# Ten one-row token tiles, a regrouped last weight and earlier row sums in an attention plus soft-MoE kernel

## The chip, the cores and the metric

The kernel runs on one core of one Trainium2 chip. The core has five engines that run side by side: TensorE (PE, with its weight loads shown apart as PEld), VectorE (DVE), ScalarE (ACT), GpSimd (POOL) and SyncE (SP), and sixteen DMA engines that carry what SP and POOL issue. The metric is the device time of one execution in microseconds (us). Four runs of the kernel before gave 177.15 to 180.34 us, median 179.23 us.

## What is computed

The reference, cut to what matters:

```python
# attention, q, k, v: (8, 8, 576, 64): scores masked to a window of 32 (heads 0-3)
# or to every 4th of 128 positions (heads 4-7), softmax, times v
x = attn_out.transpose(0, 2, 1, 3).reshape(4608, 512)
# soft mixture of experts: phi (512, 32), w1 (8, 512, 1024), w2 (8, 1024, 512)
logits = x @ phi                                # 4608 tokens x 32 slots
d = softmax(logits, axis=0); slot_input = d.T @ x           # 32 x 512
for e in range(8):                               # four slots per expert
    h = maximum(slot_input[e] @ w1[e], 0); slot_out[e] = h @ w2[e]
c = softmax(logits, axis=1)
return (c @ slot_out)                            # 4608 x 512, float32
```

The output is 4608 x 512 float32, 9.44 MB. Both softmaxes use the same exponentials: the kernel keeps exp(logits) transposed, slots by tokens (`expT`). The sum over tokens scales `slot_out` when it is evicted to `so_sb`; the sum over slots, one number per token (the row sum), becomes its reciprocal `rtok` and scales each output row.

## The kernel before

The program is a list of operations (`op(...)`), each with an engine, the buffers that it reads and writes, an estimated cost and a key. A planner (`Prog.schedule`) places them one by one: on each engine it takes, among the operations that could start within 0.1 us of the earliest, the one with the lowest key. SP and POOL keep the order in which the operations were written down. The order found so is emitted as a fixed instruction stream per engine with semaphore waits. While PE would wait within planned time 118 to 141, the planner puts in filler matmuls (line 1014) whose result nobody reads.

Eight attention units (`load_unit`, `st_T`, `st_S`, `st_V`, `st_P`, `st_X`, `st_L`) take the first 130 us or so. POOL issues their loads, and between and behind them the loads of `w1` and `w2` (`wload`, line 473), which turn float32 into bfloat16 on the way. All of these go through one software queue, in order. The second weight `w2` comes in pieces named in `W2`: (expert pair, first and last row of 16, first and last column). `p0`, `p1`, `p2` are whole pairs; the last pair is cut into `p3a` (4 rows, all 512 columns, loaded early, ahead of `p0`), `p3b` and `p3c` (the other 12 rows, columns 0 to 255) and `p3d` and `p3e` (those rows, columns 256 to 511). The last four are the last loads of the kernel.

Behind the attention PE folds the slot inputs (line 827, out of `psA_sb`), multiplies by `w1` (line 846), transposes the hidden layer (line 866) and multiplies by `w2` piece by piece as it lands (line 894), into two accumulators of 256 columns, one for each half of the output's columns. Between the `w2` pieces stand two other things: the 36 row-sum matmuls (`rsum`, line 921), one per 128 tokens, placed behind `p1` (`after=[mid]`), and seven matmuls (`keep`, line 910, `WARM = 7`) behind `p2` whose result nobody reads. When the first half's accumulator is complete, DVE scales it into `so_sb` (line 935).

The output is made in token tiles. A tile of n rows per partition has 128 n tokens, partition p holding n tokens in a row. `TILES` is (1, 2, 3, 5, 4, 8, 13). The first four tiles (`NSPLIT = 4`) are made in two halves of 256 columns: first all four with the left half, then all four with the right half; the last three take 512 columns at once. For each row PE multiplies `expT` by `so_sb` (line 972); DVE (line 991, or line 983 for two rows at once) or ACT (line 989) scales by `rtok` and evicts into a staging buffer that was a weight's home, and when all rows of a tile are there SP issues its store (line 1005). So there are 11 stores: 8 halves, whose pieces in DRAM are 256 columns long (1 KB), and three wide ones, whose pieces are a partition's whole share (8, 16 and 26 KB). SP waits at the end for all of them (line 1036).

Of the kernel before, what the change touches and what calls it, by code (L numbers as in the profile page):

```python
# [7 lines left out]
AluOp = mybir.AluOpType  # L8
# [44 lines left out]
class Op:  # L53
    n = 0
# [75 lines left out]
class Prog:  # L130
# [7 lines left out]
    def op(self, e, fn, r=(), w=(), a=(), alloc=(), cost=0.5, key=0.0, mode="f",  # L138
           sem=None, nbytes=0, nd=0, nq=1, ni=2, after=()):
        o = Op(e, fn, cost, key, mode)  # L140
        deps = list(after)
        for b in r:
            deps += b.ready
        for b in w:
            b.fresh()
            deps += b.prev
        for b in a:
            deps += b.prev
        seen = set()
        for d in deps:  # L150
            if d.id not in seen:
                seen.add(d.id)
                o.deps.append(d)
        for b in r:
            b.reads.append(o)
        for b in list(w) + list(a):
            b.ready.append(o)
        o.wr = [b for b in list(w) + list(a) if b.pool is not None]
        for b in list(r) + list(w) + list(a):
            if b.pool is not None and b not in o.touch:  # L160
                b.left += 1
                o.touch.append(b)
        o.alloc = list(alloc)
        o.sems = sem
        o.ni = ni + 2
        o.dma = nbytes / 435e3 + 0.011 * nd / 16 + 0.022 * nq
        self.ops.append(o)
        return o
# [149 lines left out]
def bass_dilated_sliding_attn__then__soft_moe_slots_kernel(  # L318
# [12 lines left out]
    op = P.op  # L331

    def sb(name, shape, dt=BF16):
        return A(nc.sbuf_tensor(name, shape, dt))

    WARM = 7
    TURNS = ((32, 0, 4), (32, 1, 4), (32, 2, 4), (16, 3, 8), (15, None, 0), (6, 39, 8), (2, None, 0),
             (2, 87, 8), (6, None, 0), (4, 103, 8), (2, 7, 8), (2, None, 0), (2, 23, 8))
    W2 = {"p3a": (3, 0, 4, 0, 512), "p0": (0, 0, 16, 0, 512), "p1": (1, 0, 16, 0, 512),
          "p2": (2, 0, 16, 0, 512), "p3b": (3, 4, 14, 0, 256), "p3c": (3, 14, 16, 0, 256),  # L340
          "p3d": (3, 4, 14, 256, 512), "p3e": (3, 14, 16, 256, 512)}
    NPT, NVN, NXB, NXT, NET = 6, 5, 5, 4, 2
    WD = sb("WD", [128, 7, 4096])
    stg = sb("stg", [128, 3, 9216])
# [40 lines left out]
    def tile(pool, size=1):  # L385
        t = Buf(pool)
        t.size = size
        return t
# [51 lines left out]
    def home(ap, al, name):  # L440
        b = Buf()
        b.al = al
        HOME[name] = (ap, b)
        b_home.append((ap, b))
# [31 lines left out]
    for e in range(7):  # L476
        home(WD[:, e, :], [], f"w1{e}")
    home(stg[:, 2, 0:4096], [b_stg[2]], "w17")
    home(stg[:, 2, 4096:6144], [b_stg[2]], "p3a")
    home(stg[:, 2, 6144:8704], [b_stg[2]], "p3b")  # L480
    home(stg[:, 0, :], [b_stg[0]], "p0")
    home(stg[:, 1, 0:8192], [b_stg[1]], "p1")
    TTf = TT[:].rearrange("p a x -> p (a x)")
# [357 lines left out]
    for hh in range(2):  # L841
        def pe(t, hh=hh):
            for c in range(4):
                for hi in range(2):
                    for j in range(4):
                        i_ = t.matmul(pair(hp)[32 * j:32 * j + 32, hh, :], siT[:, 512 * hi + 128 * c + 32 * j:
                                                       512 * hi + 128 * c + 32 * j + 32],
                                      w1v[2 * j + hi][:, c, 512 * hh:512 * hh + 512],
                                      start=(c == 0 and hi == 0), stop=(c == 3 and hi == 1))
            return i_  # L850
# [9 lines left out]
    for p_ in range(2):  # L860
# [11 lines left out]
        def ev(en, p_=p_, ht=ht):  # L872
            d_ = hT[:, 8 * p_:8 * p_ + 8, :].rearrange("p c (j i) -> p c j i", j=4)[:, :, :, 0:8]
            s_ = bank(ht)[:, 0:256].rearrange("p (c j i) -> p c j i", c=8, j=4)
            return en.activation(d_, s_, ACTF.Copy) if p_ == 0 else en.tensor_copy(d_, s_)
        op("act" if p_ == 0 else "dve", ev, r=[ht], w=[b_hT[p_]], cost=0.35, key=K1)

    TILES = []
    NSPLIT = 4
    POOLS = False  # L880
    for n in (1, 2, 3, 5, 4, 8, 13):
        TILES.append((128 * sum(x[1] for x in TILES), n))
    tok = [[expT[:, t0 + j:t0 + j + n * 127 + 1:n] for j in range(n)] for t0, n in TILES]
    rcol = [sum(n for _, n in TILES[:i]) for i in range(len(TILES))]
# [30 lines left out]
               ni=2 * WARM, key=K1 + 3.9, after=[last_])  # L915
    rs = tile(psum, 1)

    def rsum(t):
        for o, (_, n) in enumerate(TILES):
            for j in range(n):  # L920
                i_ = t.matmul(bank(rs)[:, rcol[o] + j:rcol[o] + j + 1], tok[o][j], rowm[:],
                              start=True, stop=True)
        return i_
    op("pe", rsum, r=b_expT + [b_rowm], w=[rs], alloc=[rs], cost=2.0, key=K1 + 3, ni=72,
       after=[mid])
    op("dve", lambda vv: vv.reciprocal(rtok[:], bank(rs)[:, 0:N_TOK // 128]), r=[rs], w=[b_rtok],
       cost=0.2, key=K1 + 1)

# [10 lines left out]
    for o_ in P.ops[-2:]:  # L939
# [3 lines left out]
    WDf = WD[:].rearrange("p e x -> p (e x)").bitcast(F32)  # L943
    w17f, p0f, p1f = [HOME[x][0].bitcast(F32) for x in ("w17", "p0", "p1")]
    wdh = [f"w1{e}" for e in range(7)]
    STAGE = [(w17f[:, 0:512], ["w17"]), (w17f[:, 512:1536], ["w17"]), (p0f[:, 0:1536], ["p0"]),
             (p0f[:, 1536:4096], ["p0"]), (p1f[:, 0:2048], ["p1"]), (WDf[:, 6656:10752], wdh),
             (WDf[:, 0:6656], wdh)]
    nev = 0
    for o, h_ in [(o, h_) for h_ in range(2) for o in range(NSPLIT)] + [(o, None) for o in range(NSPLIT, 7)]:  # L950
        t0, n = TILES[o]
        ost = STAGE[o][0].rearrange("p (j f) -> p j f", j=n)
        sl = slice(0, 512) if h_ is None else slice(256 * h_, 256 * h_ + 256)
        ob = Buf()
        for x in STAGE[o][1]:
            ob.prev = ob.prev + HOME[x][1].ready + HOME[x][1].reads
        k1 = K1 + 30 + o + 10 * (2 if h_ is None else h_)
        w = sl.stop - sl.start
        for j0 in range(0, n, 2):
            po = tile(psum, w // 256)  # L960
            kk = k1 + 0.1 * j0
            b_po = [Buf(), Buf()]

            def slot(j, po=po, w=w):
                if w == 512:
                    return pair(po)[:, j, :]
                return bank(po)[:, w * j:w * j + w]
            m = min(2, n - j0)
            for js in [range(m)] if w == 256 else [(j,) for j in range(m)]:
                def pe(t, o=o, slot=slot, j0=j0, js=js, sl=sl):  # L970
                    for j in js:
                        i_ = t.matmul(slot(j), tok[o][j0 + j], so_sb[:, sl], start=True, stop=True,  # L972
                                      skip_group_check=True)
                    return i_
                j = js[0]
                p0 = op("pe", pe, r=(b_so if h_ is None else b_so[h_:h_ + 1]) + b_expT, a=[po],
                        w=[b_po[j]], alloc=[po] if j == 0 else [], after=[p0] if j else [],
                        cost=0.22 if h_ is None else 0.15 * m, key=kk + 0.01 * j, ni=2 * len(js))
                col = rcol[o] + j0 + j

                def ev(en, slot=slot, ost=ost, js=js, j0=j0, sl=sl, col=col, po=po):
                    if en is nc.vector and len(js) == 2:
                        return en.tensor_tensor(
                            ost[:, j0:j0 + 2, sl], bank(po).rearrange("p (j f) -> p j f", j=2),
                            rtok[:, col:col + 2].unsqueeze(2).to_broadcast([128, 2, 256]), AluOp.mult)
                    for j in js:
                        d_, s_, sc_ = ost[:, j0 + j, sl], slot(j), rtok[:, col + j - js[0]:col + j - js[0] + 1]
                        if en is nc.scalar:
                            i_ = en.activation(d_, s_, ACTF.Copy, scale=sc_)  # L989
                        else:  # L990
                            i_ = en.tensor_scalar(d_, s_, sc_, None, op0=AluOp.mult)  # L991
                    return i_
                if w == 256:
                    o_ = op(("dve", "act"), ev, r=[b_po[j], b_rtok], a=[ob], after=ob.prev,
                            cost={"dve": 0.7 if m == 2 else 0.48, "act": 0.47 * m}, key=kk)
                else:
                    o_ = op(("dve", "act")[nev % 2], ev, r=[b_po[j], b_rtok], a=[ob], after=ob.prev,
                            cost=0.66, key=kk)
                    nev += 1
                o_.touch.append(po)  # L1000
                po.left += 1
        so = DmaSem(nc, f"s_out{o}_{h_}")
        s_out.append(so)
        op("pool" if POOLS and h_ is not None and (h_ or o > 1) else "sp",
           lambda e, t0=t0, n=n, ost=ost, sl=sl: [e.dma_start(
               out[t0:t0 + 128 * n, sl].rearrange("(p j) f -> p j f", j=n), ost[:, :, sl])],
           r=[ob], cost=0.1, sem=so, nbytes=512 * n * w, key=k1)

    def filler(n):
        t = tile(psum, 1)  # L1010
# [57 lines left out]
```

## Time and profile before

| | |
|---|---|
| median of 4 runs | 179.23 us (177.15 to 180.34) |
| profiled execution, its own time | 178.99 us |
| its span (first to last instruction) | 177.2 us |
| PE busy | 132.5 us (75%) |
| DVE busy | 113.3 us (64%) |
| ACT busy | 96.0 us (54%) |
| POOL busy | 43.5 us (25%) |
| DMA packets moved | 40.80 MB, mean 230 GB/s |
| POOL's queue (loads), share of the DMA engines | 86.7% |
| SP's queue (stores), share of the DMA engines | 13.8% |
| HBM read, written | 61.93 MB, 9.44 MB |

Positions in the profile are us from the start of the span. The profile page shows the busy share of each engine over the span in 40 slices, the chain of work that ended last, the costliest groups of instructions by line, and the DMA issues with their time to landing. Besides the page the trace answers questions on a stretch of time: the timeline (instructions merged into runs, with the idle time before them and what ended it), the busy times in given windows, the DMA issues in a window, and all instructions of one line. DMA rates count the bytes as written, so a load that turns float32 into bfloat16 counts half of what it reads. An engine's idle time costs nothing where that engine isn't the bound.

### The profile page before, as it was taken

Reading aid. Unit: us, or ns where it says so; the run is one execution under the profiler, and the core shown is the slowest. Engines: PE = TensorE matmul, PEld = TensorE weight load, DVE = VectorE, ACT = ScalarE, POOL = GpSimd, SP = SyncE. Lnnn points to the kernel's source line nnn. Section 1 sums busy time; section 2 is a strip of 40 time slices with the busy share of each in tenths; the row PEclk is TensorE's granted clock in tenths of the full one; section 3 lists DMA queues with packets and bytes.
Section 4 is the critical chain, followed back from the end, with each engine's and each line's share of the span. In section 5 each row is a group of like instructions: output and inputs, shape, how many; then the busy total and the mean of one; then the engine's idle time right before and its main releaser. Section 6 shows DMA issues by size and latency. Waiting matters only on the chain.

```text
span 177.2 us, 5828 instructions
## 1 busy us (share of the span) xinstructions
PE 132.5 (75%) x2619; PEld 104.4 (59%) x2619; DVE 113.3 (64%) x259; ACT 96.0 (54%) x144; POOL 43.5 (25%) x83
## 2 busy tenths in 40 slices
PE   0019799696999877699959999986999998695000
PEld 0019687685897676598747978875546685441000
DVE  6850388956787985887973698899550102999000
ACT  2005789584895964877853689686310100796000
POOL 7990707007004302600100590106200000000000
PEclk9999999997899999999995699999999999999655
DMA  5999999999999999999999999999999999699996
GB/s 77 202 212 220 208 218 212 219 212 211 217 212 217 219 210 211 218 216 213 214 216 215 214 211 215 217 214 232 203 214 233 194 183 174 203 341 406 456 439 288
DMA packets 11672, 40.80 MB, mean 230 GB/s; under 512 B 2176, under 2 KB 8064, under 8 KB 8192
## 3 DMA queue, kind: packets, MB, share of 16 engines
q0 software_dynamic: 7744, 30.94, 86.7%
q1 hardware_dynamic: 3904, 9.50, 13.8%
q8 instruction: 20, 0.33, 0.7%
q14 instruction: 4, 0.03, 0.0%
HBM read 61.93 MB, written 9.44 MB: 403 GB/s over the span
## 4 chain that ended last, share of the span: by engine, by line
PE 54%; DVE 18%; ACT 8%; issue 6%; DMA 5%; POOL 1%; DVEq 0%; POOLq 0%
PE ps L579 10%; PE ps L574 6%; PE ps L671 5%; PE ps L726 5%; DMA stg<-in_k_dram 5%; PE ps L617 4%; PE ps L642 4%; ACT PT L624 4%; DVE WD L991 4%; PE ps L699 4%; DVE PT L632 3%; DVE XB L682 3%; PE ps L1014 3%; DVE VN L647 3%; PE ps L757 3%
## 5 line engine op out<-in xcount | busy, mean ns | idle before, releaser
L624 ACT ACTIVATE PT<-ps 128x768 bf16<-128x768 f32 x48 | 37.2, 813 | 11.7 <-PE ps L617 11.2
L599 ACT ACTIVATE TT<-ps 128x864 f32<-128x864 f32 x32 | 28.5, 895 | 20.4 <-PE ps L579 17.6
L682 DVE TENSOR_TENSOR XB<-ps,RV 96x768 bf16<-96x768 f32 x32 | 30.4, 951 | 0.9
L579 PE MATMUL ps<-ident,stg 96*64 96x96 bf16 x576 | 19.2, 235 | 14.2 <-DMA stg<-in_k_dram 12.7
L579 PEld LDWEIGHTS ps<-ident,stg 96*64 96x64 bf16 x576 | 17.1, 132 | 15.6 <-DMA stg<-in_k_dram 12.7
L647 DVE COPY VN<-ps 128x768 bf16<-128x768 bf16 x32 | 17.0, 542 | 11.0 <-PE ps L642 11.0
L617 PE MATMUL ps<-TT 64*128 64x96 bf16 x384 | 16.3, 208 | 7.5 <-issue 4.3
L671 PE MATMUL ps<-VN,PT 128*128 128x65 bf16 x384 | 18.8, 198 | 3.4 <-issue 1.7
L430 POOL DMA_DIRECT2D stg<-in_q_dram x16 | 8.8, 549 | 42.6 <-PE ps L579 24.2
L671 PEld LDWEIGHTS ps<-VN,PT 128*128 128x128 bf16 x384 | 15.4, 101 | 5.0 <-issue 2.1
L617 PEld LDWEIGHTS ps<-TT 64*128 64x128 bf16 x384 | 10.0, 96 | 11.5 <-issue 4.6
L642 PE MATMUL ps<-ident,TT 128*128 128x128 bf16 x192 | 16.2, 226 | 0.4 <-ACT PT L624 0.4
L712 ACT ACTIVATE XT<-ps 128x576 bf16<-128x576 bf16 x22 | 13.7, 652 | 2.9 <-PE ps L699 2.9
L574 PE MATMUL ps<-ident,stg 96*128 96x96 bf16 x288 | 14.7, 206 | 0.4 <-DVE XB L682 0.4
L699 PE MATMUL ps<-ident,XB 96*128 96x96 bf16 x192 | 13.4, 216 | 1.1 <-DVE XB L682 1.1
L574 PEld LDWEIGHTS ps<-ident,stg 96*128 96x128 bf16 x288 | 13.2, 98 | 1.3 <-DVE XB L682 0.5
L632 DVE TENSOR_TENSOR PT<-PT,mask_p 128x768 bf16<-128x768 bf16 x24 | 13.0, 551 | 1.4 <-ACT PT L624 0.9
L632 DVE TENSOR_TENSOR PT<-PT,mask_d 128x768 bf16<-128x768 bf16 x24 | 12.9, 546 | 1.2 <-ACT PT L624 1.2
L642 PEld LDWEIGHTS ps<-ident,TT 128*128 128x128 bf16 x192 | 11.5, 101 | 2.4 <-ACT PT L624 0.5
L699 PEld LDWEIGHTS ps<-ident,XB 96*128 96x128 bf16 x192 | 10.2, 104 | 2.7 <-DVE XB L682 1.6
L972 PE MATMUL ps<-so_sb,expT 128*128 128x512 bf16 (+1 forms) x47 | 9.6, 334 | 2.3 <-DVE so_sb L935 1.7
L989 ACT ACTIVATE stg<-ps,rtok 128x256 f32<-128x256 f32 (+1 forms) x12 | 5.1, 513 | 10.4 <-PE ps L972 10.4
(83 smaller groups left out, 184.2 us busy)
## 6 DMA issues: line engine op xcount, KB each, us to landing
WD<-in_moe_w_dram POOLq DMA_DIRECT2D x7, 1024.0 KB, 30.4
stg<-in_q_dram POOLq DMA_DIRECT2D x16, 288.0 KB, 19.9
stg<-in_v_dram POOLq DMA_DIRECT2D x16, 288.0 KB, 20.7
stg<-in_k_dram POOLq DMA_DIRECT2D x16, 288.0 KB, 21.8
out_dram<-WD SPq DMA_DIRECT2D x1, 3328.0 KB, 12.7
stg<-in_moe_w_dram POOLq DMA_DIRECT2D x4, 512.0 KB, 19.5
stg<-in_moe_w_dram POOLq DMA_DIRECT2D x1, 2048.0 KB, 20.9
TT<-in_moe_w_dram POOLq DMA_DIRECT2D x1, 2048.0 KB, 22.1
```

The costliest lines, as they stand in the source:

```text
L574: i_ = t.transpose(bankb2(pt, a)[:, 96 * kk:96 * kk + 96], two[:, j // 2, c, :], ident[0:96, 0:96])
L579: i_ = t.transpose(bankb2(pt, a)[64 * hx:64 * hx + 64, 96 * kk:96 * kk + 96], src[:, hx, c, :], ident[0:96, 0:96])
L599: return ac.activation(d, sv, ACTF.Copy)
L617: i_ = t.matmul(pair(sc)[:, hx, QB * x:QB * x + QB], win(u, 1, h01, blk_, bpar)[64 * hx:64 * hx + 64], win(u, 0, h01, blk_, bpar)[64 * hx: ...
L624: op("act", lambda ac: ac.activation(sbt(pt)[:, 0:768].rearrange("p (x n) -> p x n", x=2), pair(sc)[:, :, 0:384], ACTF.Exp, scale=SCALE), ...
L632: return dv.tensor_tensor(p_, p_, m.unsqueeze(1).to_broadcast([128, 2, 384]), AluOp.mult)
L642: i_ = t.transpose(bankb(pv)[:, 128 * m:128 * m + 128], win(u, 2, h01, m, bpar), ident[:, :])
L647: op("dve", lambda dv: dv.tensor_copy(sbt(vn)[:, :, :, 0:64], bankb(pv)[:, 0:768].rearrange("p (m x d) -> p m x d", m=6, x=2)), r=[pv], w= ...
L671: i_ = t.matmul(pair(po)[:, bk, 65 * po_:65 * po_ + 65], sbt(pts[i])[:, o_:o_ + 128], sbt(vn)[:, m, half, 0:65], start=True, stop=True)
L682: op("dve", lambda dv: dv.tensor_tensor(sbt(xb)[:].rearrange("p m (x h d) -> p h x m d", x=2, h=2)[:, h01], pv()[:, :, :, 0:64], sbt(rv)[: ...
L699: i_ = t.transpose(bankb(px)[:, QB * m:QB * m + QB], sbt(xb)[:, m, 128 * x:128 * x + 128], ident[0:QB, 0:QB])
L712: return en.activation(d, s_, ACTF.Copy)
```

## The change

Four edits, all at the end of the kernel:

1. `W2`: `p3a` takes 6 rows of the last pair instead of 4, in its early load; `p3b` and `p3d` have 8 rows instead of 10. `p3c` and `p3e` stay at 2 rows. So ten rows instead of twelve come in the two loads of each 256-column half.
2. The row sums are three operations of 12 matmuls with key `K1 - 5`, below the key of the slot input fold (`K1`), and no longer wait for `mid`; they are ready as soon as the last `expT` is.
3. `WARM` is 2 instead of 7.
4. `TILES` is ten tiles of one row and then 3, 8 and 15 rows (`NSPLIT = 10`). The ten are made in two halves as before, so there are 20 stores of 128 KB and then three wide ones: 23 instead of 11. Tiles 0 and 1 stand alone; the others go in pairs that share a PSUM bank and one eviction operation, which evicts both with two instructions on one engine (line 983's form, one DVE instruction for two rows, is gone). Each tile has its own store.

The diff, cut to its core:

```diff
-    WARM = 7
+    WARM = 2
-    W2 = {"p3a": (3, 0, 4, 0, 512), "p0": (0, 0, 16, 0, 512), "p1": (1, 0, 16, 0, 512),
-          "p2": (2, 0, 16, 0, 512), "p3b": (3, 4, 14, 0, 256), "p3c": (3, 14, 16, 0, 256),
-          "p3d": (3, 4, 14, 256, 512), "p3e": (3, 14, 16, 256, 512)}
+    W2 = {"p3a": (3, 0, 6, 0, 512), "p0": (0, 0, 16, 0, 512), "p1": (1, 0, 16, 0, 512),
+          "p2": (2, 0, 16, 0, 512), "p3b": (3, 6, 14, 0, 256), "p3c": (3, 14, 16, 0, 256),
+          "p3d": (3, 6, 14, 256, 512), "p3e": (3, 14, 16, 256, 512)}
...
-    NSPLIT = 4
-    POOLS = False
-    for n in (1, 2, 3, 5, 4, 8, 13):
+    NSPLIT = 10
+    for n in NSPLIT * (1,) + (3, 8, 15):
         TILES.append((128 * sum(x[1] for x in TILES), n))
...
-    op("pe", rsum, r=b_expT + [b_rowm], w=[rs], alloc=[rs], cost=2.0, key=K1 + 3, ni=72,
-       after=[mid])
+    cols = [(rcol[o] + j, tok[o][j]) for o, (_, n) in enumerate(TILES) for j in range(n)]
+    for i0 in range(0, 36, 12):
+        def rsum(t, i0=i0):
+            for c, l_ in cols[i0:i0 + 12]:
+                i_ = t.matmul(bank(rs)[:, c:c + 1], l_, rowm[:], start=True, stop=True)
+            return i_
+        op("pe", rsum, r=b_expT + [b_rowm], a=[rs], alloc=[rs] if i0 == 0 else [], cost=0.65, key=K1 - 5, ni=24)
...
+    def store(o, sl, b, key):
+        t0, n = TILES[o]
+        so = DmaSem(nc, f"s_out{o}_{sl.start}")
+        s_out.append(so)
+        op("sp", lambda e: [e.dma_start(
+            out[t0:t0 + 128 * n, sl].rearrange("(p j) f -> p j f", j=n), ost[o][:, :, sl])],
+            r=[b], cost=0.1, sem=so, nbytes=512 * n * (sl.stop - sl.start), key=key)
+
+    def scaled(en, d_, s_, c):
+        if en is nc.scalar:
+            return en.activation(d_, s_, ACTF.Copy, scale=rtok[:, c:c + 1])
+        return en.tensor_scalar(d_, s_, rtok[:, c:c + 1], None, op0=AluOp.mult)
+
+    for h_ in range(2):
+        sl = slice(256 * h_, 256 * h_ + 256)
+        for os in [(0,), (1,)] + [(o, o + 1) for o in range(2, NSPLIT, 2)]:
+            po = tile(psum, 1)
+            kk = K1 + 30 + 10 * h_ + 0.1 * os[0]
+
+            def pe(t, os=os, po=po, sl=sl):
+                for j, o in enumerate(os):
+                    i_ = t.matmul(bank(po)[:, 256 * j:256 * j + 256], tok[o][0], so_sb[:, sl],
+                                  start=True, stop=True, skip_group_check=True)
+                return i_
+            op("pe", pe, r=b_so[h_:h_ + 1] + b_expT, w=[po], alloc=[po], cost=0.15 * len(os), key=kk,
+               ni=2 * len(os))
+            obs = [staged(o) for o in os]
+
+            def ev(en, os=os, po=po, sl=sl):
+                for j, o in enumerate(os):
+                    i_ = scaled(en, ost[o][:, 0, sl], bank(po)[:, 256 * j:256 * j + 256], o)
+                return i_
+            op(("dve", "act"), ev, r=[po, b_rtok], a=obs, after=[x for b in obs for x in b.prev],
+               cost=0.47 * len(os), key=kk)
+            for o, b in zip(os, obs):
+                store(o, sl, b, kk)
     nev = 0
-    for o, h_ in [(o, h_) for h_ in range(2) for o in range(NSPLIT)] + [(o, None) for o in range(NSPLIT, 7)]:
+    for o in range(NSPLIT, len(TILES)):
...
```

The wide tiles are made as before, one 512-column matmul and one eviction per row, DVE and ACT in turn, and then one store. The staging buffers are cut anew for the new tiles.

More of the change, by code (lines that the diff above doesn't have):

```diff
@@ L478, in bass_dilated_sliding_attn__then__soft_moe_slots_kernel @@
     home(stg[:, 2, 0:4096], [b_stg[2]], "w17")
-    home(stg[:, 2, 4096:6144], [b_stg[2]], "p3a")
-    home(stg[:, 2, 6144:8704], [b_stg[2]], "p3b")
+    home(stg[:, 2, 4096:7168], [b_stg[2]], "p3a")
+    home(stg[:, 2, 7168:9216], [b_stg[2]], "p3b")
     home(stg[:, 0, :], [b_stg[0]], "p0")
@@ L916, in bass_dilated_sliding_attn__then__soft_moe_slots_kernel @@
     rs = tile(psum, 1)
[L918 to L923, printed above, removed]
-    op("pe", rsum, r=b_expT + [b_rowm], w=[rs], alloc=[rs], cost=2.0, key=K1 + 3, ni=72,
-       after=[mid])
+    cols = [(rcol[o] + j, tok[o][j]) for o, (_, n) in enumerate(TILES) for j in range(n)]
[5 more added lines that the diff above has]
+        op("pe", rsum, r=b_expT + [b_rowm], a=[rs], alloc=[rs] if i0 == 0 else [], cost=0.65, key=K1 - 5, ni=24)
     op("dve", lambda vv: vv.reciprocal(rtok[:], bank(rs)[:, 0:N_TOK // 128]), r=[rs], w=[b_rtok],
@@ L945, in bass_dilated_sliding_attn__then__soft_moe_slots_kernel @@
     wdh = [f"w1{e}" for e in range(7)]
-    STAGE = [(w17f[:, 0:512], ["w17"]), (w17f[:, 512:1536], ["w17"]), (p0f[:, 0:1536], ["p0"]),
-             (p0f[:, 1536:4096], ["p0"]), (p1f[:, 0:2048], ["p1"]), (WDf[:, 6656:10752], wdh),
-             (WDf[:, 0:6656], wdh)]
-    nev = 0
-    for o, h_ in [(o, h_) for h_ in range(2) for o in range(NSPLIT)] + [(o, None) for o in range(NSPLIT, 7)]:
[L951 to L960, printed above, removed]
+    STAGE = [(w17f[:, 512 * i:512 * i + 512], ["w17"]) for i in range(4)]
@@ new lines, in bass_dilated_sliding_attn__then__soft_moe_slots_kernel, with staged @@
+    STAGE += [(p0f[:, 512 * i:512 * i + 512], ["p0"]) for i in range(NSPLIT - 4)]
+    STAGE += [(p1f[:, 0:1536], ["p1"]), (WDf[:, 7680:11776], wdh), (WDf[:, 0:7680], wdh)]
+    ost = [t.rearrange("p (j f) -> p j f", f=512) for t, _ in STAGE]
+    def staged(o):
+        b = Buf()
+        for x in STAGE[o][1]:
+            b.prev = b.prev + HOME[x][1].ready + HOME[x][1].reads
+        return b
+    def store(o, sl, b, key):
[5 more added lines that the diff above has]
+            r=[b], cost=0.1, sem=so, nbytes=512 * n * (sl.stop - sl.start), key=key)
@@ L961, in bass_dilated_sliding_attn__then__soft_moe_slots_kernel @@
+    nev = 0
+    for o in range(NSPLIT, len(TILES)):
+        ob = staged(o)
+        k1 = K1 + 50 + o
+        for j0 in range(0, TILES[o][1], 2):
+            po = tile(psum, 2)
             kk = k1 + 0.1 * j0
             b_po = [Buf(), Buf()]
[L964 to L999, printed above, removed]
@@ new lines, in bass_dilated_sliding_attn__then__soft_moe_slots_kernel @@
+            for j in range(min(2, TILES[o][1] - j0)):
+                p0 = op("pe", lambda t, o=o, po=po, j=j, j0=j0: t.matmul(
+                    pair(po)[:, j, :], tok[o][j0 + j], so_sb[:], start=True, stop=True),
+                    r=b_so + b_expT, a=[po], w=[b_po[j]], alloc=[po] if j == 0 else [],
+                    after=[p0] if j else [], cost=0.22, key=kk + 0.01 * j)
+                o_ = op(("dve", "act")[nev % 2], lambda en, o=o, po=po, j=j, j0=j0: scaled(
+                    en, ost[o][:, j0 + j, :], pair(po)[:, j, :], rcol[o] + j0 + j),
+                    r=[b_po[j], b_rtok], a=[ob], after=ob.prev, cost=0.66, key=kk)
+                nev += 1
@@ L1000, in bass_dilated_sliding_attn__then__soft_moe_slots_kernel @@
                 o_.touch.append(po)
                 po.left += 1
[L1002 to L1007, printed above, removed]
+        store(o, slice(0, 512), ob, k1)
     def filler(n):
```

## The prediction

> **What bounds the kernel now.** The page's chain of work names PE for 54% and then DVE evictions, but it follows instructions, and the last 12 us of the span have none: SP only waits for a store to land. So I read the tail in windows (columns: stretch; busy us and count of PE, PEld, DVE, ACT, POOL; granted clock; DMA share; GB/s).
>
> ```profile
> 151.20:151.80 0.60, 0.60 (x16) 0.41 (x13) 0.60 (x2) 0.60 (x3) 0.00 (x0) 1.00 0.00 0
> 153.00:160.50 7.50, 6.84 (x32) 3.54 (x33) 7.12 (x13) 6.88 (x14) 0.00 (x0) 1.00 1.02 342
> 161.00:163.00 2.00, 0.96 (x3) 0.24 (x3) 2.00 (x4) 1.58 (x3) 0.00 (x0) 1.00 1.00 415
> 168.00:176.00 8.00, 0.00 (x0) 0.00 (x0) 0.00 (x0) 0.00 (x0) 0.00 (x0) 0.50 0.99 426
> ```
>
> From 153 to 176 the DMA engines are full: 342 GB/s while the 256-column halves go out in 1 KB pieces, 415 for the four-row tile, 426 for the largest. Before that, 151.2 to 151.8 moves nothing: the loads are through and no store has begun. So the end is set by **when stores begin to fill the DMA engines, and then by 9.44 MB at these rates.** The timeline shows what the first store waits for.
>
> ```profile
> 146.46 1.06 PE L894 MATMUL ps<-TT,hT 128*32 128x256 bf16 x32
> 147.45 1.69 PE L910 MATMUL ps<-mask_p,ident 128*128 128x512 bf16 x7
> 149.06 0.51 PE L894 MATMUL ps<-stg,hT 128*32 128x256 bf16 x10
> 149.66 0.48 DVE L935 TENSOR_SCALAR so_sb<-ps,rcs 128x256 bf16<-128x256 f32 x1 [2.71 <-PE ps L894]
> 150.52 0.48 DVE L991 TENSOR_SCALAR stg<-ps,rtok 128x256 f32<-128x256 f32 x1 [0.38 <-PE ps L972]
> 151.03 7.52 SPq L1005 DMA_DIRECT2D out_dram<-stg  x9
> ```
>
> The first half's last weight piece, p3c, is issued at 122.72 and lands 24.6 later, at 147.3:
>
> ```profile
> TT<-in_moe_w_dram POOLq DMA_DIRECT2D x1, 128.0 KB, 24.6
> ```
>
> PE stands at that moment in front of the seven matmuls of line 910 and comes to p3b and p3c only at 149.06. So 1.7 us of the path are PE's own order, not the weights; from the eviction to `so_sb` (149.66) to the first store are 1.37 us.
>
> **The change part by part.** The sum is made on the profiled execution: 178.99 us, of which 177.2 are span and 1.8 lie around it. The last store is issued at 164.11 and lands 12.7 later, 176.8; its bytes are through at 176.05 (no rate after 176). It stands 0.24 under the median of the four runs.
>
> *Row sums, moved ahead of the fold.* They leave 1.91 us (36 matmuls, 144.62) and take the same in thirds of 0.64 between 130 and 133, where PE runs fillers: 0.66 us in front of the last slot matmuls and 0.97 in front of the fold (line 1014 in the chain of waits). Two thirds fit; the third may push the fold back by 0.3 to 0.65. That is hidden: the `w2` work of p3a, p0, p1 then ends at 145.3 at the latest instead of 144.6, p2 (1.06) at 146.4, the two matmuls left of line 910 (2 x 0.23) at 146.9, all before p3b lands. DVE makes `rtok` earlier, and nothing waits for that. The sums hold one of eight PSUM banks for some 3 us more. If the cover were gone, the price is at most the 0.65.
>
> *WARM.* Five matmuls of 0.23 us go, 1.2 us, from in front of p3b. With the row sums gone too, PE is no longer late; next late is **p3c's landing**.
>
> *The weight pieces.* p3a grows by two rows of 512 columns, 256 KB as written. p1 and p2 land 9.65 us apart (133.65, 143.3) for 2048 KB, so all behind p3a moves by 1.21. p3b takes 3.35 us for ten rows (143.3 to 146.65), so eight save 0.67: p3c lands at 147.3 + 1.21 - 0.67 = 147.85. p3e saves 0.67 once more: 151.65 becomes 151.5. POOL issues as many loads as before. From landing to PE's start I take 0.1 (between 0 and the 0.42 of idle before line 894's first load at 142.53); p3c's two matmuls need 0.3, so the eviction to `so_sb` starts at 148.35 instead of 149.66. **The first store is issued at 151.03 - 1.3 = 149.73.**
>
> *Matmuls and evictions of the halves.* 20 rows of 256 columns instead of 22. DVE loses its two-row form (0.62 us a pair, start to start) for 2 x 0.43; ACT needs 0.39 a row. Both together make a row in 0.21 us, and a row's store is 0.38 us of DMA time (131,072 B at 342 GB/s), so evictions stay ahead: pairs (2,3) and (4,5) are ready at about 150.5 and 150.6, when SP has just issued two stores. The second half's `so_sb` needs p3e (151.5, say 152.1 when its last bytes share the engines with stores), 0.35 of matmuls, 0.48 of eviction: rows from 153.9. SP needs until then for the first ten stores. Costed at nothing.
>
> *The stores.* This is the new item: 20 issues on SP in place of 8 for the halves. The two one-row stores of before are the nearest rows:
>
> ```profile
> L1005 SPq DMA_DIRECT2D out_dram<-stg x1: 348/348/348, 151.0 to 151.0; - x1
> L1005 SPq DMA_DIRECT2D out_dram<-stg x1: 463/463/463, 153.9 to 153.9; - x1
> ```
>
> The first found the queue empty, the second some seven rows in flight. Between two issues SP takes 0.05 (to 0.12 with a wait of its own: 152.21 to 152.33). So one store per 0.40 to 0.51 us against 0.38 of DMA time: SP, not the DMA engines, sets the pace, barely. The other end is the two-row store's 0.61 (it alone has two rows' pieces), 0.66 with the gap; below 0.38 the DMA engines decide. With about three rows in flight (1.25 us from issue to last byte, below) I take 0.35 + 3/7 x 0.115 = 0.40, and 0.45 with the gap.
>
> A one-row store's bytes are through 1.25 us after its issue (151.03; the engines begin at 151.9, plus 0.38). The 20th is issued at 149.73 + 19 x 0.45 = 158.3 and through at 159.55. The wide part then follows without a hole: before 1.05 MB / 415 + 2.10 / 426 + 3.41 / 426 = 2.53 + 4.92 + 8.00 = 15.45; after 0.79 / 415 + 2.10 / 426 + 3.93 / 426 = 1.90 + 4.92 + 9.23 = 16.05, because two rows more go wide. Its evictions are done at about 164.0 as now (26 rows at 0.33 from 155.4), the 15-row store's bytes can start at 165, and the eight-row tile runs until 166.4: covered by 1.4 us. Last byte 159.55 + 16.05 = 175.6 instead of 176.05, **0.45 less: 178.99 - 0.45 = 178.5.**
>
> Where the Trainium skill speaks against this: "DMA: Bandwidth & Descriptors", section Measured, asks for 1 MiB a transfer and calls small ones dominated by descriptors; interpolated in its table a 128 KB transfer alone takes about 1.3 us (an estimate), 26 us for twenty. In this trace stores of 128 to 640 KB behind one another hold 342 GB/s, the one-row store at 153.92 among them, so its fixed part overlaps, and I keep to the rows.
>
> Against fewer filler matmuls, the trace first: after 2.1 us without matmuls (91.3 to 93.4) the granted clock is 0.50 for some 7 us.
>
> ```profile
> 92.00:94.00 2.00, 0.61 (x10) 0.52 (x10) 0.00 (x0) 0.30 (x2) 0.00 (x0) 0.88 1.02 212
> 94.00:96.00 2.00, 2.00 (x43) 1.74 (x41) 0.92 (x2) 0.63 (x2) 0.00 (x0) 0.50 1.04 215
> ```
>
> After the change PE's longest holes are about 0.5 us on either side of p3b and later 1 us for the second half. Were the clock halved, a 512-column matmul would take 0.43 instead of 0.22 us against 0.33 of eviction per row: 16 in 7 us, 1.6 us late, against 1.4 us of cover, and 0.2 for the first row. At most 0.4, taken as 0. The skill ("TensorE: Matmul & The Clock Gate", Part 1) names a window of about 3.4 us of idleness; by it no hole here would count, while the 2.1 us of this trace leaves less room, and the measurement decides.
>
> **The rivals.**
>
> *The halves stay DMA-bound (the whole gain).* If an issue stays at 0.35 plus 0.05, the 20th store goes out at 157.33, is through at 158.6, and the end is 174.65: 1.4 us less, 177.6. With no issue limit, bytes from 150.6 on and 7.67 us for 2.62 MB give 158.3, 177.3. For it: the queue is short, as it was at the first store. Against: the second one-row store.
>
> *SP's issues become the bound (slower).* The period p decides from 149.73 + 19p + 1.25 + 16.05 = 176.05, p = 0.475 us: each further 0.05 us costs 0.95 us. At 0.51 it is 179.6, at 0.66 182.5. For it: issues under way beside 1 KB traffic took 463 to 1150 ns (the one-row store the least). Against: those long ones stood behind a deep queue, where SP's wait costs nothing.
>
> *The first store isn't earlier.* If the planner's new order puts PE behind p3c again, or the fold is pushed back by more than the 1.0 us or so of slack, the start stays at 151.03: 1.3 lost, 179.8 at p = 0.45.
>
> **How the numbers follow.** Forecast 178.5 (p between 0.43 and 0.475, 178.1 to 179.0): 0.40. Whole gain, 177.3 to 178.1: 0.27. Issue-bound, 179.0 to 182.5: 0.25. No earlier start, 179 to 180.5: 0.08. Range 176.9 to 181.0: it leaves out the issue-bound cases with p above 0.58 and takes in 0.4 below the whole gain for the spread of the runs. A measurement of this kernel tells a difference of about 2% (3.6 us) from no change; none of the gains reaches that, the issue-bound end just does: faster 0.03, same 0.90, slower 0.07.
>
> **What would show it.** In the changed profile: line 894's p3b and p3c right at their landing (about 148), the first store at 149.7, no window without DMA traffic between 150.6 and the end, SP's one-row stores 0.45 us apart, the halves' last bytes at about 159.5, the last store issued near 164 with the eight-row tile still going out. I'm wrong if stores stand 0.5 us or more apart while the DMA share is under 0.9, if PE is held before 148 by something other than p3c, or if the 15-row tile's evictions end after 165.4.

## The result, and the profile after

The changed kernel is slower: median 179.5 us (43 runs, 178.83 to 183.13) against 178.6 us for the kernel before (64 runs); the ratio is 1.0087, 95% interval 1.0066 to 1.0107, or 1.55 us. The ratios, here and below, leave out the runs that lie more than 1.5% above the fastest of their kernel. Forecast was 0.45 us less. The change is under the 2% that the prediction counts as telling, but its interval leaves out 1. The first profiled execution of the changed kernel (183.13 us) was the slowest of its 43, so the profile shown here is a second one, of run e1_after (180.29 us, span 178.6).

The windows of the tail, with the columns of those shown of before (stretch; busy us and count of PE, PEld, DVE, ACT, POOL; granted clock; DMA share; GB/s):

```profile
151.00:151.60 0.60, 0.60 (x14) 0.32 (x11) 0.60 (x2) 0.60 (x3) 0.00 (x0) 1.00 0.00 0
152.50:160.50 8.00, 7.14 (x30) 3.20 (x31) 7.62 (x15) 7.18 (x16) 0.00 (x0) 1.00 0.81 268
168.00:176.00 8.00, 0.00 (x0) 0.00 (x0) 0.00 (x0) 0.00 (x0) 0.00 (x0) 0.50 1.01 432
```

The empty stretch around 151 is still there, and behind it the DMA engines are no longer full: 0.81 busy at 268 GB/s where before had 1.02 at 342. The wide stores run at 432 (before: 426). The timeline ahead of the first store, and all store issues by line (duration min/median/max in ns):

```profile
144.67 2.36 PE L893 MATMUL ps<-stg,hT 128*32 128x256 bf16 x76
147.50 1.06 PE L893 MATMUL ps<-TT,hT 128*32 128x256 bf16 x32
148.49 0.61 PE L909 MATMUL ps<-mask_p,ident 128*128 128x512 bf16 x2
149.03 0.40 PE L893 MATMUL ps<-stg,hT 128*32 128x256 bf16 x8
149.57 0.48 DVE L933 TENSOR_SCALAR so_sb<-ps,rcs 128x256 bf16<-128x256 f32 x1 [5.12 <-PE ps L893]
150.95 1.81 SPq L959 DMA_DIRECT2D out_dram<-stg  x4
```

```profile
L959 SPq DMA_DIRECT2D out_dram<-stg x21: 349/447/456, 150.9 to 160.8; - x21
L959 SPq DMA_DIRECT2D out_dram<-WD x2: 333/362/390, 161.2 to 163.9; - x2
```

Two things went otherwise than the sum. PE comes to p3b at 149.03, as late as before (149.06), though the row sums and five matmuls are gone from in front of it: the first store goes out at 150.95 and not at 149.73. And SP's one-row stores take 0.45 us each, all but the first two within 10 ns of it, 0.49 with the gap: the 20th is issued at 160.18, 9.23 behind the first, where 8.55 were forecast.

Why PE is late is read from the granted clock (the third column from the right) around the fold. The changed kernel:

```profile
132.00:134.00 2.00, 2.00 (x18) 1.94 (x18) 1.07 (x2) 0.00 (x0) 0.00 (x0) 0.59 1.15 246
136.00:138.00 2.00, 2.00 (x24) 0.79 (x20) 0.00 (x0) 0.00 (x0) 0.00 (x0) 0.50 0.77 164
```

The kernel before:

```profile
132.00:134.00 2.00, 2.00 (x10) 1.44 (x10) 0.69 (x1) 0.00 (x0) 0.00 (x0) 1.00 1.15 246
136.00:138.00 2.00, 2.00 (x44) 0.97 (x36) 0.00 (x0) 0.60 (x1) 0.00 (x0) 1.00 0.84 180
```

PE is shown busy for the whole of these windows in both, but in the changed kernel the clock falls to half at 132.4, for 6.8 us, while the last of the early row sums run (130.37 to 132.8). The `w1` matmuls (line 846) then start from 135.62 to 140.61, 5.0 us from the first to the last instead of 3.3. The fold starts at 132.76 here and at 132.79 in the profile of before, and the first store follows 18.2 us later in both: 3.1 us of PE work were taken out of that stretch, and the half clock (1.7 in the `w1` matmuls, 0.4 between fold and `w1`) and, for the rest, four more matmuls for the larger `p3a`, small holes and a filler in front of `p2` took their place.

### The profile page after: what moved, and what is told of

Same layout as the page of the kernel before. It is cut to its first block, busy times and chain, and to the rows that moved or that the text cites. A ratio compares the mean times of both kernels' runs of the same rounds, so it can differ in the third digit from the quotient of the medians.

```text
span 181.4 us, 5822 instructions
## 1 busy us (share of the span) xinstructions
PE 137.7 (76%) x2608; PEld 107.8 (59%) x2608; DVE 113.4 (62%) x261; ACT 96.8 (53%) x145; POOL 43.4 (24%) x83
## 4 chain that ended last, share of the span: by engine, by line
PE 55%; DVE 19%; ACT 6%; issue 5%; DMA 5%; POOL 1%; DVEq 0%; POOLq 0%
PE ps L579 9%; PE ps L642 6%; PE ps L574 6%; PE ps L617 5%; PE ps L726 5%; PE ps L671 5%; DMA stg<-in_k_dram 5%; PE ps L699 4%; DVE WD L966 4%; DVE XB L682 4%; DVE stg L966 3%; PE ps L846 3%; DVE VN L647 3%; DVE PT L632 3%; ACT TT L599 3%
## 5 line engine op out<-in xcount | busy, mean ns | idle before, releaser
L579 PEld LDWEIGHTS ps<-ident,stg 96*64 96x64 bf16 x576 | 17.2, 132 | 15.3 <-DMA stg<-in_k_dram 12.8
L617 PE MATMUL ps<-TT 64*128 64x96 bf16 x384 | 17.3, 222 | 6.0 <-issue 3.7
L642 PE MATMUL ps<-ident,TT 128*128 128x128 bf16 x192 | 18.6, 245 | 0.4 <-ACT PT L624 0.3
L617 PEld LDWEIGHTS ps<-TT 64*128 64x128 bf16 x384 | 10.9, 103 | 10.1 <-issue 4.2
L642 PEld LDWEIGHTS ps<-ident,TT 128*128 128x128 bf16 x192 | 13.2, 110 | 2.8 <-ACT PT L624 0.4
L574 PEld LDWEIGHTS ps<-ident,stg 96*128 96x128 bf16 x288 | 13.7, 100 | 0.8 <-issue 0.2
L680 DVE RECIPROCAL RV<-ps 96x12 f32<-96x12 f32 x32 | 7.2, 223 | 6.1 <-PE ps L671 5.9
L726 PE MATMUL ps<-XT,phi_pad 128*128 128x192 bf16 (+1 forms) x64 | 9.9, 301 | 0.2 <-DVE expX L738 0.2
## 6 DMA issues: line engine op xcount, KB each, us to landing
out_dram<-WD SPq DMA_DIRECT2D x1, 3840.0 KB, 14.2
```

The lines of the kernel that those rows point to most:

```text
L574: i_ = t.transpose(bankb2(pt, a)[:, 96 * kk:96 * kk + 96], two[:, j // 2, c, :], ident[0:96, 0:96])
L579: i_ = t.transpose(bankb2(pt, a)[64 * hx:64 * hx + 64, 96 * kk:96 * kk + 96], src[:, hx, c, :], ident[0:96, 0:96])
L617: i_ = t.matmul(pair(sc)[:, hx, QB * x:QB * x + QB], win(u, 1, h01, blk_, bpar)[64 * hx:64 * hx + 64], win(u, 0, h01, blk_, bpar)[64 * hx: ...
L642: i_ = t.transpose(bankb(pv)[:, 128 * m:128 * m + 128], win(u, 2, h01, m, bpar), ident[:, :])
L726: i_ = t.matmul(o_, phi_pad[:, c].rearrange("p j i -> p (j i)"), rhs, start=c == 0, stop=c == 3)
```

## The experiments

Theory S: SP's 0.49 us per issue, longer than the 0.38 us of DMA time that a one-row store holds, sets the pace of the halves. Rival F: what was moved ahead of the stores costs. After the first four runs F was made into theory C (the thin row sums in the place of dense filler matmuls halve the clock) with rival W (the missing matmuls of line 910 do). All ratios are to the kernel before on the same chip.

**e1_after: the changed kernel again.** No edit.

> The changed kernel itself, again, for an undisturbed profile and as the mark for the others. Theory S (SP's issues set the pace of the one-row stores, 0.49 us each as in the first profile of the changed kernel, against 0.38 of DMA time): 0.9% slower than before, first store about 1.3 us earlier than the 151.0 of before, 20 stores 0.49 apart, DMA share about 0.8 among them. Rival F (what was moved ahead of the stores costs: the row sums, the missing matmuls of line 910, the weight pieces): the same 0.9%, but the first store at 151 or later.

Measured 1.0102 (1.0064 to 1.0141). Store spacing and DMA share are as S has them, the first store is at 151 as F has it. Both are needed.

**e2_tiles: the tiles and stores alone.** The changed kernel with the other three edits taken back.

```diff
-    WARM = 2
+    WARM = 7
-    W2 = {"p3a": (3, 0, 6, 0, 512), "p0": (0, 0, 16, 0, 512), "p1": (1, 0, 16, 0, 512),
+    W2 = {"p3a": (3, 0, 4, 0, 512), "p0": (0, 0, 16, 0, 512), "p1": (1, 0, 16, 0, 512),
...
-        op("pe", rsum, r=b_expT + [b_rowm], a=[rs], alloc=[rs] if i0 == 0 else [], cost=0.65, key=K1 - 5, ni=24)
+    op("pe", rsum, r=b_expT + [b_rowm], w=[rs], alloc=[rs], cost=2.0, key=K1 + 3, ni=72,
+       after=[mid])
```

> Only the tiles and their stores of the change; the row sums, seven matmuls of line 910 and the weight pieces are as before. Theory S: first store at 151.0 as before, last one-row store 19 x 0.49 later, bytes through 1.25 after that, then 16.05 of wide stores: 177.6 in place of 176.05, so 1.6 us or 0.9% slower. Rival F: no slower than 0.2%.

Measured 1.0073 (1.0020 to 1.0126), 1.3 us: the tiles alone make most of the loss. The stores stand 0.49 apart here too, and the DMA engines have holes among them:

```profile
150.50:158.50 8.00, 6.50 (x36) 3.70 (x37) 6.18 (x12) 5.23 (x11) 0.00 (x0) 0.79 0.85 278
```

**e3_front: the front alone.** The kernel before with the other three edits.

```diff
-    WARM = 7
+    WARM = 2
-    W2 = {"p3a": (3, 0, 4, 0, 512), "p0": (0, 0, 16, 0, 512), "p1": (1, 0, 16, 0, 512),
+    W2 = {"p3a": (3, 0, 6, 0, 512), "p0": (0, 0, 16, 0, 512), "p1": (1, 0, 16, 0, 512),
...
-    op("pe", rsum, r=b_expT + [b_rowm], w=[rs], alloc=[rs], cost=2.0, key=K1 + 3, ni=72,
-       after=[mid])
+        op("pe", rsum, r=b_expT + [b_rowm], a=[rs], alloc=[rs] if i0 == 0 else [], cost=0.65, key=K1 - 5, ni=24)
```

> Only what stands ahead of the stores: row sums in thirds, two matmuls of line 910, the new weight pieces; tiles and stores as before. Theory S: the first store 1.3 us earlier and the stores bound by the DMA engines as before, so 1.3 us or 0.7% faster than before. Rival F: 0.5 to 0.9% slower than before.

Measured 1.0016 (0.9962 to 1.0070). Neither expectation: no cost stands clear of the noise (by the medians of all runs, 179.39 against 178.47 us, it is 0.5% slower), but the gain of 0.7% that the sum has for it isn't there either. Its profile has the clock at 0.56 from 132 to 134 like the changed kernel's:

```profile
132.00:134.00 2.00, 1.78 (x10) 1.16 (x15) 0.29 (x1) 0.00 (x0) 0.00 (x0) 0.56 0.93 197
```

Here the half clock holds nothing up: the fold starts at 131.08, 1.7 us earlier than in e1, p3c lands at 147.89, and the first store goes out at 149.64, as close behind p3c as the sum has it.

**e4_pairs: one store for two tiles.**

```diff
-            for o, b in zip(os, obs):
-                store(o, sl, b, kk)
+            if len(os) == 2:
+                store2(os[0], sl, obs, kk)
+            else:
+                store(os[0], sl, obs[0], kk)
...
+        op("sp", lambda e: [e.dma_start(
+            out[128 * o:128 * o + 256, sl].rearrange("(j p) f -> p j f", p=128),
+            src.rearrange("p (j f) -> p j f", f=512)[:, :, sl])],
```

> The changed kernel with one store for each pair of one-row tiles (the same pieces of 1 KB, bytes, staging and evictions; 12 stores in place of 20). Theory S: an issue of two rows takes 0.61 + 0.05 us for 0.77 of DMA time, so the DMA engines are full again: 1.5 to 2 us faster than the changed kernel and 0.5 to 1% faster than before. Rival F: as the changed kernel, 0.9% slower than before.

Measured 0.9992 (0.9948 to 1.0036): 1.1% or 1.9 us under the changed kernel, as S has it, with the same bytes in the same 1 KB pieces. Against before the gain is missing, as in e3. The halves' window, and the pair stores:

```profile
153.50:160.50 7.00, 5.87 (x26) 2.82 (x27) 6.62 (x14) 6.18 (x13) 0.00 (x0) 1.00 1.00 331
```

```profile
L967 SPq DMA_DIRECT2D out_dram<-stg x8: 448/498/722, 153.1 to 158.2; - x8
```

An issue of two rows costs hardly more at the median than one of one row (0.50 against 0.45), and the DMA engines are full again.

**e5_pool: half of the one-row stores by POOL.**

```diff
-        op("sp", lambda e: [e.dma_start(
+        op("pool" if n == 1 and o % 2 else "sp", lambda e: [e.dma_start(
```

> The changed kernel with the odd ones of the ten one-row tiles stored by POOL's queue instead of SP's; same 23 stores, pieces and bytes. Theory S (SP's 0.49 us per issue): two queues issue side by side, the DMA engines are full, 1.3 to 2 us faster than the changed kernel, as with the pair stores, so about as fast as before. Rival: many small stores are slow in the DMA engines themselves, whoever issues them: 265 GB/s and 1.0% slower than before still.

Measured 1.0011 (0.9967 to 1.0055). Every other engine's instructions are those of the changed kernel. 23 stores are no burden for the DMA engines (0.98 busy); one queue's issues are.

```profile
151.00:158.50 7.50, 6.17 (x28) 2.89 (x29) 6.62 (x14) 6.09 (x13) 4.49 (x9) 1.00 0.98 317
L959 SPq DMA_DIRECT2D out_dram<-stg x11: 332/448/1124, 149.6 to 156.6; - x11
L959 POOL DMA_DIRECT2D out_dram<-stg x10: 540/540/602, 150.0 to 155.7; - x10
```

SP's one-row issues are not of one length here: they take 0.33 us after a pause and up to 0.82 us where two queues keep the DMA engines full (the 1.12 is the three-row tile). As SP no longer sets the pace, that costs nothing.

**e6_warm: two matmuls of line 910 alone.** In the kernel before:

```diff
-    WARM = 7
+    WARM = 2
```

> The kernel before with two matmuls of line 910 instead of seven, nothing else. Theory C (what halves the granted clock from about 132 on is the row sums in the place of dense filler matmuls in front of the fold; the front of the change gives that time back): no half clock between 130 and 145, PE on p3b 1.1 us earlier, stores DMA-bound, 0.9 to 1.1 us or 0.5% faster than before. Rival W (the missing matmuls of line 910 cost the clock): half clock at about 148 to 152 and no gain.

Measured 0.9989 (0.9955 to 1.0023), the clock full from 130 to 145. Rival W falls. But 0.1% is not the 0.5% that freeing PE by 1.1 us should bring, and the interval excludes 0.5%.

**e7_rsum: the row sums alone.** In the kernel before:

```diff
-    op("pe", rsum, r=b_expT + [b_rowm], w=[rs], alloc=[rs], cost=2.0, key=K1 + 3, ni=72,
-       after=[mid])
+        op("pe", rsum, r=b_expT + [b_rowm], a=[rs], alloc=[rs] if i0 == 0 else [], cost=0.65, key=K1 - 5, ni=24)
```

> The kernel before with the row sums alone moved ahead of the fold, in thirds. Theory C: half clock for 3.4 to 6.8 us somewhere from 130 to 142, the w1 matmuls 4 to 5 us long instead of 3.3, a mean granted clock some 0.015 lower than before; the 1.9 us that leave the place behind p1 are given back, so within 0.3% of before. Rival W: clock as before, the first store about 1.5 us earlier, 0.8% faster.

Measured 1.0111 (1.0045 to 1.0177), worse than C had it. The clock is at half from 132.1 on for 6.8 us, the `w1` matmuls take 4.4 us, and the first store goes out at 152.26. Six runs are few, and in the profiled one the fold itself starts at 133.81, a microsecond later than in the profile of before.

**e8_w2: the weight pieces alone.** In the kernel before:

```diff
-          "p2": (2, 0, 16, 0, 512), "p3b": (3, 4, 14, 0, 256), "p3c": (3, 14, 16, 0, 256),
+          "p2": (2, 0, 16, 0, 512), "p3b": (3, 6, 14, 0, 256), "p3c": (3, 14, 16, 0, 256),
...
-    home(stg[:, 2, 4096:6144], [b_stg[2]], "p3a")
+    home(stg[:, 2, 4096:7168], [b_stg[2]], "p3a")
```

> The kernel before with the new weight pieces alone. Where PE arrives at p3b before p3c has landed (the fold at about 131 rather than 133), p3c lands 0.55 us later (147.9 instead of 147.3) and pushes the first store by as much; where PE arrives late, nothing changes: 0.1 to 0.3% slower than before. Rival: the pieces are worth the 0.15 us by which p3e lands earlier, 0.1% faster.

Measured 1.0053 (1.0014 to 1.0092). p3c lands at 147.96 there, and the first store goes out at 149.71. The sign is the expected one, the size larger.

**e9_sums_back: the changed kernel with its row sums behind p1 again.**

```diff
-        op("pe", rsum, r=b_expT + [b_rowm], a=[rs], alloc=[rs] if i0 == 0 else [], cost=0.65, key=K1 - 5, ni=24)
+    op("pe", rsum, r=b_expT + [b_rowm], w=[rs], alloc=[rs], cost=2.0, key=K1 + 3, ni=72,
+       after=[mid])
```

> The changed kernel with the row sums back in one piece behind p1, all else as changed (two matmuls of line 910, new weight pieces, ten one-row tiles). Theory C: no half clock from 130 to 142, mean clock as before (0.928), first store about 1 us earlier than in the changed kernel; the stores still 0.49 us apart, so 0.3 to 0.5% slower than before and 0.5 to 0.7% faster than the changed kernel. Rival W: clock and time as the changed kernel, 1.0% slower than before.

Measured 1.0082 (1.0045 to 1.0118). The clock is full from 130 to 142 and the first store stands at 149.58, as C has it, but the ratio is only 0.2% under that of e1_after, taken on another chip, or 0.05% under that of the 43 runs, and the intervals overlap: what the early row sums cost in the time of the changed kernel isn't told from nothing. Eight of its twelve runs lie between 178.89 and 179.12: with SP's twenty issues behind it, an early first store ends there.

**e11_dense: dense matmuls among the early row sums.**

```diff
             for c, l_ in cols[i0:i0 + 12]:
+                if c % 4 == 0:
+                    t.matmul(bank(dn)[:, 0:512], ident[:, :],
+                             mask[0][:].rearrange("p m x -> p (m x)")[:, 0:512],
+                             start=True, stop=True)
                 i_ = t.matmul(bank(rs)[:, c:c + 1], l_, rowm[:], start=True, stop=True)
```

> The changed kernel with nine 512-column matmuls whose result nobody reads put among the 36 early row sums, one ahead of every four: 1.9 us more PE work in front of the fold. Theory C: the granted clock stays full from 130 to 142, the w1 matmuls take 3.3 us, and the mean clock is near that of before (0.928); what they cost at the fold they give back behind it, so the time is within 0.3% of the changed kernel. Rival (the place of the row sums, not their thinness, costs the clock): half clock from about 133 on all the same, 0.8% slower than the changed kernel.

Measured 1.0100 (1.0048 to 1.0152), as the changed kernel. The place of the row sums is the same, the work in front of the fold is more, and the clock stays full. The first store follows the fold by 15.3 us (134.70 to 150.03) and not by 18.2. The dense matmuls start the fold 1.9 us later than in e1, so only 0.9 us of that is left at the first store, and the ratio shows nothing of it:

```profile
132.00:134.00 2.00, 2.00 (x29) 1.54 (x22) 0.69 (x1) 0.00 (x0) 0.00 (x0) 1.00 1.00 213
136.00:138.00 2.00, 2.00 (x26) 1.12 (x29) 0.29 (x1) 0.00 (x0) 0.00 (x0) 1.00 0.73 156
```

The `w1` matmuls of before, of the changed kernel and of this one (ns each, min/median/max, first and last start):

```profile
L846 PE MATMUL ps<-WD,siT x56: 379/379/390, 135.2 to 138.5; 128*32 128x512 bf16 x56
```

```profile
L846 PE MATMUL ps<-WD,siT x56: 379/538/634, 135.6 to 140.6; 128*32 128x512 bf16 x56
```

```profile
L846 PE MATMUL ps<-WD,siT x56: 379/379/390, 137.1 to 140.3; 128*32 128x512 bf16 x56
```

Over the profiles of all runs, those below included, the clock from 130 to 142 is 0.72 to 0.86 in all six with early row sums and nothing dense among them, and 1.00 in the other eleven. The mean clock over whole executions is noisier: in the first four runs' timed executions 0.910 to 0.914 with early sums against 0.931 in e2, here 0.928, but 0.917 in e9.

**b1_before, b2_before, b3_before: the unchanged kernel.** No edit. Open was why e6 and e3 gain so little.

> The kernel before, unchanged, another profile. If the first profile had a late PE: in some of these three the fold starts at 130.5 to 131.5, PE is through line 910 before p3c lands, and the first store goes out at 149.1 to 149.4, without any change. If something else holds the store: 151.0 again in all three.

> As the run before it: first store at 149.1 to 149.4 where the fold starts before 131.5, at fold + 18.2 where it starts later; 151.0 in all three if something else holds it.

> As the two before it: first store at 149.1 to 149.4 where the fold starts before 131.5, at fold + 18.2 where it starts later; 151.0 in all three if something else holds it.

Measured 179.06, 179.06 and 177.06 us. In the first two the fold starts at 132.9 and the first store at 151.1, as in the profile that the prediction was made on. In the third the fold starts at 130.3, and PE waits for the weights:

```profile
144.93 1.69 PE L910 MATMUL ps<-mask_p,ident 128*128 128x512 bf16 x7
146.79 0.51 PE L894 MATMUL ps<-stg,hT 128*32 128x256 bf16 x10 [0.17 <-DMA stg<-in_moe_w_dram]
147.43 0.10 PEld L894 LDWEIGHTS ps<-TT,hT 128*32 128x32 bf16 x2 [0.42 <-DMA TT<-in_moe_w_dram]
149.14 2.52 SPq L1005 DMA_DIRECT2D out_dram<-stg  x4
```

The seven matmuls of line 910 are through by 146.6, p3b and p3c are taken as they land (the weight loads of the last two matmuls wait 0.42 for p3c), and the first store is at 149.14 without any change. The kernel has two kinds of execution, about 2 us apart: of 29 runs of before beside e5, e8, e11 and e12, 16 lie at 176.9 to 177.8 and 13 at 178.8 to 181.2. The division is not always so clean: of the 64 runs of before beside the other experiments, 15 lie between these groups. In the first kind, as b3 shows it, there was nothing to gain in front of the first store. I call the two early and late, by the fold.

**e10_pairs_back and e12_best: what the runs point to.** The edits of e4_pairs and e9_sums_back together; e12 also takes the weight pieces of before:

```diff
-          "p2": (2, 0, 16, 0, 512), "p3b": (3, 6, 14, 0, 256), "p3c": (3, 14, 16, 0, 256),
+          "p2": (2, 0, 16, 0, 512), "p3b": (3, 4, 14, 0, 256), "p3c": (3, 14, 16, 0, 256),
```

> Both causes taken away: one store for each pair of one-row tiles, and the row sums back behind p1; the rest as changed. Theory C with SP's issues as the other cause: first store about 149.9, DMA-bound from there, 0.6 to 0.9% faster than before. Rival W: as the pair stores alone, no faster than before.

> What the runs so far point to: one-row tiles with pair stores, two matmuls of line 910, row sums behind p1 and the weight pieces of before. p3c lands at 147.3 again, first store about 149.2, DMA-bound from there: 0.4 to 0.8% faster than before. If the weight pieces don't matter: as with the new pieces, 0.3% faster.

Measured 0.9972 (0.9936 to 1.0009) and 0.9966 (0.9922 to 1.0011). Both are 1.1 to 1.4% under the changed kernel; neither is told from before by its interval. The 0.4 to 0.9% that were expected rest on the late kind of execution, so they are mostly missing. In the late kind the gain is there: the profile of e12 is one (fold at 132.64), and its first store goes out at 149.78, 1.25 us before that of before. Between the two the weight pieces make no difference that shows, unlike in e8.

## Why the prediction was wrong, step by step

- *What bounds the kernel now.* Right for the kernel before (weights, first store, then bytes), but read from one execution of the late kind. "1.7 us of the path are PE's own order, not the weights" holds in two of the three further profiles; in the third PE's order costs nothing, and p3c's landing is the bound already.
- *Row sums, "hidden ... the price is at most the 0.65".* **This step failed.** The push on the fold that was priced did not come: in e1 the fold starts 0.05 us behind the last addition into `psA_sb` (132.71 to 132.76), as before (132.73 to 132.79). What wasn't priced came: with one-column matmuls in the place of 512-column ones the clock fell to half. Price in e1: 1.7 us in the `w1` matmuls and 0.4 between them and the fold. The prediction looked for a half clock beside p3b, where PE would be idle and where the clock stays full in e1, and not where PE is busy with thin matmuls. e7 has the half clock and a loss by this edit alone; e11 takes the half clock away with dense matmuls in the same place, though its ratio shows no gain. The `w2` work of p3a, p0 and p1, forecast to end at 145.3 at the latest, ended at 147.0 in e1. In the profiles this price reaches the first store in late executions only: in e3 and e5 the clock is at half too, but the folds start at 131.08 and 130.29, and the first stores go out at 149.64 and 149.62, right behind p3c.
- *WARM.* The 1.2 us are gone from PE, and the clock doesn't mind (e6). What they bring is 0.1%. p3c's landing is next late, as the step says, and in the early executions, about half of them, it was the bound before.
- *The weight pieces.* p3c at 147.85 forecast, 147.93 measured. Costed as part of a gain, since PE was taken to be late; where PE is early, the later landing is a loss (0.5% alone).
- *"The first store is issued at 149.73."* Measured 150.95 in e1. 1.2 us of the miss in that execution. In early ones (e3, e5, and e9 with its sums back) it is 149.58 to 149.64, as forecast, but there the kernel before has 149.14 (b3): no gain in either kind, where 1.3 us were counted.
- *The stores, p = 0.45.* The mechanism was named and its break-even (0.475) too; **the term was mis-sized.** The interpolation by rows in flight was wrong: in e1 the issue takes 0.35 once, 0.43 for the second and then 0.45, with about four stores under way (0.49 apart, 1.9 us from issue to landing; the sum had three), hardly less than the 0.46 that was read with seven rows in flight. With the gap it is 0.49. 19 x 0.49 - 19 x 0.45 is 0.7 us, and it turned the forecast's side. The stores' part can be read apart from where they begin: from the first store's issue to the last landing it is 27.15 or 27.16 us in e1, e2, e9 and e11, 25.74 to 25.76 in all four profiles of before, and 25.2 to 25.3 with the pair stores of e4, e10 and e12. So the one-row stores lose 1.4 us, in early and late executions alike, where the sum has 0.86 (149.73 to 176.35); that is most of the 1.55 us. Issued in pairs, the same tiles are 0.5 us shorter than before. The rival on the other side is what happened, at p = 0.49.
- *The wide part.* 16.05 us against 15.45, covered by its evictions: the 15-row store was issued at 163.94 with the eight-row tile still going out, and landed 14.2 later, at 178.1. Forecast was 175.6 + 0.75 = 176.35. The difference is 1.75 us; the two terms above make 1.9, so nothing is left for others.

The Trainium skill ("DMA: Bandwidth & Descriptors", section Measured) calls transfers under 64 KB dominated by their descriptors. The one-row stores have 128 KB, so that rule doesn't reach them, and the prediction set it aside by the rate of 342 GB/s, rightly: e5 keeps the engines 0.98 busy with the same stores. The page also says, in its section Issuing engines are not separate DMA queues, that the time to initiate a DMA is usually small beside the DMA itself. Here the issue period is 0.49 us against 0.38 us of the DMA engines' time, and that was the bound.

What stays open: why some executions reach the fold 2 us later than others. The half-clock spells of the first 125 us differ between profiles (20.5 us in b2, 10.2 us in b3, but 10.2 us also in the first profile of before, which was late), so their sum alone doesn't say it. Why the weight pieces cost 0.5% in e8 and nothing between e10 and e12 wasn't followed further. And that the width of the matmuls is what the clock follows is inferred from e11, which also adds 1.9 us of work; other widths weren't tried.

## What to carry to other kernels

Before a store is cut into more pieces, compare the issue period of one queue, measured with several identical issues in a row, with the DMA time of one piece: below that size the queue is the bound, and fewer, larger issues or a second queue give the time back. Before filler matmuls are replaced by useful ones, compare how wide they are, and look for the effect in the matmuls behind them, not in PE's busy time. And where a kernel's runs fall into two groups, take profiles of both before a gain is counted from one of them.

## What was not expected of the hardware

- PE shown busy nearly all the time (5.8 of the 6.0 us from 126 to 132 in e1) can lose its clock: 36 one-column matmuls with full weight loads among short work were followed by 3.4 to 6.8 us at half clock in six profiles of six, and nine 512-column matmuls among them kept it at 1.00.
- One behind another, issues on SP cost more by the issue than by the row: 0.45 us for 128 pieces of 1 KB (e1), 0.50 at the median (0.45 to 0.72) for 256 (e4). POOL's issues of the same stores took 0.54 to 0.60 us and ran beside SP's.
